# Score bounds from five multiply-adds on VectorE instead of five small matmuls, with a column step of five in Wq and Wk

## The chip, the cores and the metric

The kernel runs on one core of a Trainium2 chip. The metric is the time of one execution in microseconds (us), taken as the median of several runs. A core has five engines with queues of their own: TensorE (PE in the profile, its weight loads PEld), VectorE (DVE), ScalarE (ACT), GpSimd (POOL) and SyncE (SP), which here does nothing but issue DMAs. Each queue is worked off in order; between queues only semaphores order the work.

## The reference, cut to what matters

A block with segmented linear memory beside a softmax attention, gated by a GLU. B = 1, S = 2048, D = 640, H = 32 heads of Dh = 20, four segments of L = 512 tokens, GLU width 1536.

```
xn = layernorm(x)
q, k, v = heads(xn @ wq), heads(xn @ wk), heads(xn @ wv)
for each segment s of 512 tokens:
    logits = q_s k_s^T * Dh**-0.5 + mask           # causal mask of -1e9
    a_dot  = softmax(logits) v_s
    a_mem  = phi(q_s) M / (phi(q_s) z + 1e-6)      # phi(t) = t+1 if t > 0 else exp(t)
    o      = g * a_mem + (1 - g) * a_dot           # g = sigmoid(beta), one per head
    M, z   = M + phi(k_s)^T v_s, z + sum(phi(k_s))
s = concat(o) @ wo
g = silu( (sigmoid(xn @ w_gate) * (xn @ w_up)) @ w_down )
out = x + s * g
```

The kernel subtracts from each score a bound of its query instead of the row's maximum: for a query q and a head, the sum over the head's 20 features of |q_d| times the largest |k_d| in the segment. The bound is the same for all keys of a query, so the softmax does not change; it only keeps the exponential from overflowing.

## The kernel before, in words

**Tiling.** Everything is held transposed, with features on the 128 partitions and 512 tokens along a row: xnT is 5 chunks of 128 features. Per segment, `proj` (L283) makes K and Q in five tiles of 128 features x 512 tokens each, five matmuls a tile, evacuated to bf16 by ScalarE or VectorE into `ktd` and `qtd` (L292 to L301). V is made with tokens on the partitions (L347). The GLU is 12 gate tiles and 12 up tiles (L420, L431) and eight down tiles (L443).

**Scores.** A head has 20 features, so four heads go side by side: `KT` and `QT` hold, at partitions 32r to 32r+19, the features of head 4g+r, for eight groups g. As the features of a head straddle the 128-feature chunks, K and Q go out to DRAM (`spill`, L303, into Kd and Qd) and come back in that layout (`relayout`, L310, four DMAs of 20 partitions a half; half 0 is groups 0 to 3, half 1 groups 4 to 7). A unit of `scores` (L545) is up to 512 columns for four heads at once, four row strips of TensorE; its PSUM tile Sps is single. One exponential on ScalarE (L556) reads it, GpSimd masks the diagonal (L558), `attend_T` (L562) multiplies by V, and VectorE and GpSimd divide (the "turn", L580 to L593). There are 80 units, 20 a segment; the text calls the stretch from one unit to the next a slot.

**The bound.** Three rows at partitions 32r+20 to 32r+22 of QT carry the negative bound in three parts, against three rows of ones in KT, so that the scores' matmul (23 rows deep) subtracts it. `do_K` takes the largest |k| of each feature over the 512 tokens (`kabs`, L295). `q_abs` clears the sign bits of Q (`aq`, L320, in two calls). `bound` (L323) multiplies an indicator of heads, `Ind`, by kabs (`ik`, L326). `bound_mm` (L330) runs five matmuls of 32 output columns, ik against aq, into the PSUM tile `cps`, ScalarE copies it to `cb` (L338), and a DMA puts it into DRAM (Bd, L339). `bound_dma` (L341) brings the three rows back into QT, four DMAs a half.

**Memory.** phi of Q and of the transposed K (`ktok`, a DMA transpose of Kd, L377) is made in place by `phi_min`, `phi_exp`, `phi_end` (L361 to L375): two VectorE instructions, an exponential on ScalarE, an addition on VectorE. phi(Q) is needed from segment 1 on, for `mem_part` (L402), whose blocks of M lie in the order of the natural features.

**Order.** Everything is put in order by hand. `TIMES` gives for each piece of a segment the slot (0 to 20) at which it is issued, and the main loop issues, slot by slot, scores and exponentials, then the events due in this slot, filled up between them with GLU matmuls (`fill`, `step`) so that the work per slot is even. An event carries its TensorE time; that of `bound_mm` is C_NS. In slots ahead of an `attend_T`, matmuls are issued as four of 32 output columns each (`mm`, L134 instead of L130), which run side by side. All PSUM tiles but Sps come from one pool of four buffers. Segment m = n+1 has its K, Q, V and bounds made in slots 9.75 to 20 of segment n; segment 0 has them made ahead of the first slot, written out at the end of the set-up code.

## Time and profile before

| what | value |
|---|---|
| median of 3 runs | 319.95 us (319.74 to 320.09) |
| profiled execution: span from the first to the last instruction | 317.6 us |
| what lies around that span in the median run | 2.35 us |
| first unit of scores (start of the first slot) | 35.68 us |
| first unit of segments 1, 2, 3 | 102.6, 169.1, 235.9 us |
| granted TensorE clock over the span | 0.999 |
| ScalarE's exponentials (L556) | 81, 1.86 us each |

The profile is of one execution on the chip. A group's line gives the source line, the engine, the operation, out<-in with partitions x elements, the count, then busy time and the mean of one in ns, then the engine's idle time just before those instructions and what ended most of it. The waits view names who waited for whom, in us in total, times and the longest. The timeline gives start, duration and line; "SPq" rows are DMAs being issued, not moved. When a DMA has landed is told by its semaphore's marks in the trace.

### The profile page before, as it was taken

To read this page: it belongs to the slowest core of one execution; us is meant where nothing else is said; L and a number is where in the kernel's file an instruction comes from. 1 tells how busy PE (TensorE), PEld (TensorE's weight loads), DVE (VectorE), ACT (ScalarE), POOL (GpSimd) and SP (SyncE) were. 2 spreads that over 40 slices of the span, in tenths; PEclk is the share of its full clock that TensorE was granted. 3 is DMA by queue.
4 is the path that set the end of the run, shared out by engine and by line. 5 is a ranking of instruction groups with operands and counts; after the bars stand their busy time and mean duration, and the time that the engine had idled before them with its cause. 6 is when DMAs were issued, how large, how long until landed. Compare 5 with 4: busy or idle time off the path is not lost.

```text
span 317.6 us, 10049 instructions
## 1 busy us (share of the span) xinstructions
PE 309.7 (98%) x4215; PEld 167.1 (53%) x4244; DVE 229.5 (72%) x505; ACT 227.2 (72%) x229; POOL 135.5 (43%) x230
## 2 busy tenths in 40 slices
PE   8999999999999999999999999999999999999995
PEld 3544445665555445654665455545466645445673
DVE  6474356755869888997779999977787686734565
ACT  3723477788898877778898868678897766777631
POOL 1870036535263445334453354444533353535322
PEclk9999999999999999999999999999999999999999
DMA  7984886420752462505954443238533000350302
GB/s 252 364 328 142 289 221 191 105 46 2 215 158 62 130 130 85 126 23 173 240 168 122 114 110 109 82 121 210 168 82 120 19 23 23 114 137 4 99 20 83
DMA packets 56085, 41.36 MB, mean 130 GB/s; under 512 B 26952, under 2 KB 54664, under 8 KB 56040
## 3 DMA queue, kind: packets, MB, share of 16 engines
q1 hardware_dynamic: 53496, 35.97, 39.7%
q10 hardware_dynamic: 2544, 4.75, 4.0%
q8 instruction: 33, 0.54, 0.7%
q14 instruction: 12, 0.10, 0.1%
HBM read 19.90 MB, written 14.78 MB: 109 GB/s over the span
## 4 chain that ended last, share of the span: by engine, by line
PE 96%; issue 1%; ACT 1%; DVE 1%; ACTq 0%
PE yp L130 11%; PE up L130 11%; PE gp L130 10%; PE psq L130 10%; PE Sps L548 9%; PE gp L134 6%; PE up L134 6%; PE yp L134 6%; PE psv L130 6%; PE ApsT L572 5%; PE psq L134 4%; PE sp L130 3%; PE sp L134 3%; PE sp L532 2%; PE psv L134 1%; PE wps L644 1%
## 5 line engine op out<-in xcount | busy, mean ns | idle before, releaser
L556 ACT ACTIVATE pt<-Sps 128x2048 bf16<-128x2048 f32 (+1 forms) x81 | 150.3, 1856 | 40.8 <-PE Sps L548 35.9
L558 POOL TENSOR_SCALAR_AFFINE_SELECT pt<-pt 128x512 bf16<-128x512 bf16 x128 | 83.2, 665 | 157.6 <-ACT pt L556 157.5
L438 DVE SCALAR_TENSOR_TENSOR hT<-tg,up 128x512 bf16<-128x512 bf16 x48 | 32.4, 675 | 23.2 <-PE up L130 8.7
L130 PE MATMUL up<-xnT,Wu 128*128 128x512 bf16 x147 | 40.3, 380 | 1.2 <-issue 1.0
L130 PE MATMUL yp<-Wd,hT 128*128 128x320 bf16 x257 | 40.1, 300 | 0.0
L427 ACT ACTIVATE tg<-gp 128x512 bf16<-128x512 f32 x48 | 28.6, 596 | 14.4 <-PE gp L130 11.0
L130 PE MATMUL gp<-xnT,Wg 128*128 128x512 bf16 x144 | 38.1, 379 | 0.3 <-issue 0.2
L548 PE MATMUL Sps<-QT,KT 23*128 23x128 bf16 (+3 forms) x512 | 32.6, 301 | 0.2
L591 DVE STREAM_TRANSPOSE obT<-ob 128x512 bf16<-128x512 bf16 x30 | 21.1, 705 | 13.4 <-POOL ob L587 13.3
L130 PEld LDWEIGHTS <-hT 128*128 128x128 bf16 x257 | 23.5, 98 | 11.6 <-issue 3.0
L455 DVE SCALAR_TENSOR_TENSOR aa<-t,yp 128x320 bf16<-128x320 bf16 x32 | 15.3, 480 | 13.8 <-ACT t L454 13.7
L134 PE MATMUL gp<-xnT,Wg 128*32 128x512 bf16 x360 | 24.1, 380 | 0.0
L548 PEld LDWEIGHTS <-KT 23*128 23x128 bf16 x512 | 10.0, 92 | 24.5 <-issue 24.1
L130 PEld LDWEIGHTS <-Wu 128*128 128x128 bf16 x160 | 14.3, 98 | 16.2 <-issue 3.2
L593 DVE STREAM_TRANSPOSE tb<-ApsT 128x512 f32<-128x512 f32 x30 | 21.2, 708 | 2.2 <-PE ApsT L572 2.1
L572 PE MATMUL ApsT<-pt,V 128*32 128x512 bf16 (+2 forms) x480 | 22.7, 299 | 0.0
L130 PEld LDWEIGHTS <-Wg 128*128 128x128 bf16 x150 | 14.1, 98 | 16.0 <-issue 1.9
L134 PE MATMUL up<-xnT,Wu 128*32 128x512 bf16 x320 | 21.7, 380 | 0.0
L454 ACT ACTIVATE t<-yp 128x320 bf16<-128x320 f32 x32 | 13.9, 435 | 10.2 <-PE yp L130 8.5
L130 PE MATMUL psv<-Wv,xnT 128*128 128x320 bf16 x130 | 20.6, 299 | 0.2
L587 POOL TENSOR_TENSOR ob<-tb,rb 128x320 bf16<-128x320 f32 x27 | 19.8, 733 | 2.3
L134 PE MATMUL yp<-Wd,hT 128*32 128x320 bf16 x508 | 20.0, 300 | 0.0
(122 smaller groups left out, 448.7 us busy)
## 6 DMA issues: line engine op xcount, KB each, us to landing
KT<-Kd SPq DMA_DIRECT2D x32, 80.0 KB
QT<-Qd SPq DMA_DIRECT2D x32, 80.0 KB
out_dram<-xt SPq DMA_DIRECT2D x14, 160.0 KB
Wg<-in_B_w_gate_dram ACTq DMA_DIRECT2D x1, 1920.0 KB
Wu<-in_B_w_up_dram ACTq DMA_DIRECT2D x1, 1920.0 KB
xt<-in_A_x_dram SPq DMA_DIRECT2D x3, 640.0 KB
Wd<-in_B_w_down_dram SPq DMA_DIRECT2D x1, 1920.0 KB
Xd<-xn SPq DMA_DIRECT2D x12, 160.0 KB
```

The lines of the kernel that those rows point to most:

```text
L130: nc.tensor.matmul(out_, lhsT=lhsT, rhs=rhs, start=start, stop=stop, skip_group_check=True)
L134: nc.tensor.matmul(out_[cols], lhsT=lhsT[:, cols], rhs=rhs, start=start, stop=stop, tile_position=(0, 32 * r), skip_group_check=True)
L427: nc.scalar.activation(tg[:], gp[:], ACT.Tanh, scale=0.5)
L438: nc.vector.scalar_tensor_tensor(out=h[:], in0=seg[n]["tg"][:], scalar=1.0, in1=up[:], op0=ALU.add, op1=ALU.mult)
L455: nc.vector.scalar_tensor_tensor(out=s["aa"][j][:, hs], in0=t2[:], scalar=1.0, in1=yp[:], op0=ALU.add, op1=ALU.mult)
L548: nc.tensor.matmul(Sps[:, r, c0:c0 + ncol], lhsT=KT[32 * r:32 * r + DH + 3, g, kb * P:(kb + 1) * P], rhs=QT[32 * r:32 * r + DH + 3, g, q0: ...
L556: nc.scalar.activation(pt[:, :, 0:ntot], Sps[:, :, 0:ntot], ACT.Exp, scale=SCALE)
L558: nc.gpsimd.affine_select(out=pt[:, :, c0:c0 + P], in_=pt[:, :, c0:c0 + P], compare_op=ALU.is_ge, fill=0.0, base=0, pattern=[[0, 4], [1, P ...
L572: nc.tensor.matmul(ps[32 * r:32 * r + 32, q0:L], lhsT=Vflat[n % 2][:, off:off + 32], rhs=t[:, r, c0:c0 + ncol], start=(i == 0), stop=(i == ...
L587: nc.gpsimd.tensor_tensor(ob[:, :, 0:DH], tb[:, :, 0:DH], rb[:].unsqueeze(2).to_broadcast([P, L // 32, DH]), op=ALU.mult)
L591: nc.vector.transpose(s["obT", g // 4][:, g % 4, :], ob[:].rearrange("p b e -> p (b e)"))
L593: s["turn", g] = (lambda: nc.vector.transpose(tb[:].rearrange("p b e -> p (b e)"), ps[:]), quotients, turn_back)
```

## The change

- `proj` reads Wq and Wk with a column step of five: tile c holds the features 5p + c at partition p, not 128c + p. So the 20 features of a head lie on four partitions, five to each, all five tiles alike.
- `bound` becomes five VectorE instructions, issued in four events: cb = aq[0] * kmax[0], then four times cb = aq[c] * kmax[c] + cb, each 128 x 512 with the scalar taken per partition. `Ind`, `ik`, the five matmuls, the PSUM tile `cps` and ScalarE's copy go. Each head has four bound rows now, one for each of its four partitions; KT's unused rows are -1 instead of 1, and the scores' matmul is 24 rows deep.
- K and Q are each written out whole, in one DMA (five rows of 1 KB at a stretch for each partition), after their last tile, and not in two parts. In DRAM the features stand in natural order.
- From segment 1 on, Q is read back in natural order (`q_again`, 128 partitions of five rows of 1 KB) into a new `qtd` for phi, so phi of Q begins a little later.
- The order of the DMAs on SP changes accordingly: Q out, K out, bounds out, Q back, then the relayouts. In the set-up code Q now goes out after its fifth tile instead of three tiles after the third.

```diff
-    q_spill1=15.26, k_spill1=17.0, q_abs=(13.5, 14.79), bound=14.78, bound_mm=15.9, ...
-    phi_q=((16.0, 16.6, 17.12), (18.3, 18.7, 19.18)),
+    q_spill=14.3, k_spill=14.95, k_lay0=15.5, q_lay0=16.33, q_again=15.3, q_abs=(13.5, 14.79), bound=(14.5, 14.7, 15.0, 15.2),
+    phi_q=((16.4, 17.0, 17.5), (18.3, 18.7, 19.18)),
...
-        nc.gpsimd.memset(KT[:].bitcast(mybir.dt.uint32), 0x3F803F80)
+        nc.gpsimd.memset(KT[:].bitcast(mybir.dt.uint32), 0xBF80BF80)
...
-            mm(ps[:], W[:, k, c * P:(c + 1) * P], xnT_of[n][:, k, :], k == 0, k == DC - 1)
+            mm(ps[:], W[:, k, :].rearrange("p (m c) -> p c m", c=DC)[:, c, :], xnT_of[n][:, k, :],
+               k == 0, k == DC - 1)
...
+    def spill(n, dd, key, eng):
+        eng.dma_start(dd[n % 2][:].rearrange("(m c) n -> m c n", c=DC), seg[n][key][:])
+
+    def q_again(n):
+        seg[n]["qt"] = stg.tile([P, DC, L], BF, name="qtd")
+        nc.sync.dma_start(seg[n]["qt"][:], Qd[n % 2][:].rearrange("(c p) n -> p c n", p=P))
...
+    def bound(n, c0, c1):
+        s = seg[n]
+        if c0 == 0:
+            s["cb"] = stg.tile([P, L], BF, name="cb")
+        for c in range(c0, c1):
+            kmax = s["kabs"][:, c:c + 1]
+            if c == 0:
+                nc.vector.tensor_scalar(s["cb"][:], s["aq"][:, c, :], kmax, None, op0=ALU.mult)
+            else:
+                nc.vector.scalar_tensor_tensor(out=s["cb"][:], in0=s["aq"][:, c, :], scalar=kmax, in1=s["cb"][:],
+                                               op0=ALU.mult, op1=ALU.add)
+        if c1 == DC:
+            nc.sync.dma_start(Bd[n % 2][:], s["cb"][:])
...
-            nc.sync.dma_start(QT[32 * r + DH:32 * r + DH + 3, 4 * half:4 * half + 4, :],
+            nc.sync.dma_start(QT[32 * r + DH:32 * r + DH + 4, 4 * half:4 * half + 4, :],
...
-    for c in range(5):
+    for c in range(DC):
         do_K(0, c, nc.vector)
+    spill(0, Kd, "kt", nc.sync)
+    for c in range(DC):
+        do_Q(0, c, nc.scalar)
         if c == 2:
-            spill(0, 0, nc.sync, None)
-    for c in range(3):
-        do_Q(0, c, nc.scalar)
-    q_abs(0, 0, 3)
-    spill(0, 0, None, nc.sync)
+            q_abs(0, 0, 3)
+            bound(0, 0, 3)
     relayout(0, 0, Kd, KT, nc.sync)
-    relayout(0, 0, Qd, QT, nc.sync)
-    for c in range(3, 5):
-        do_Q(0, c, nc.scalar)
+    spill(0, Qd, "qt", nc.sync)
     q_abs(0, 3, DC)
-    bound(0)
+    bound(0, 3, DC)
     finish(do_gate(0, 0))
     finish(do_up(0, 0))
-    bound_mm(0)
+    relayout(0, 0, Qd, QT, nc.sync)
     bound_dma(0, 0)
```

More of the change, by code (lines that the diff above doesn't have):

```diff
@@ L70 @@
     K_eng='vaava', Q_eng='avvav', V=(10.3, 13.3, 14.4, 14.6, 16.35, 17.45, 19.75, 19.85), V_eng='avaavvav',
-    k_spill0=14.77, k_lay0=15.15, q_spill0=14.1, q_lay0=16.33, q_spill1=15.26, k_spill1=17.0, q_abs=(13.5, 14.79), bound=14.78,
-    bound_mm=15.9, bound_lay0=18.6, load_x=14.7, phi_k=((7.08, 7.78, 8.23), (12.7, 12.8, 13.7)),
-    phi_q=((16.0, 16.6, 17.12), (18.3, 18.7, 19.18)),
+    q_spill=14.3, k_spill=14.95, k_lay0=15.5, q_lay0=16.33, q_again=15.3, q_abs=(13.5, 14.79), bound=(14.5, 14.7, 15.0, 15.2),
+    bound_lay0=18.6, load_x=14.7, phi_k=((7.08, 7.78, 8.23), (12.7, 12.8, 13.7)),
+    phi_q=((16.4, 17.0, 17.5), (18.3, 18.7, 19.18)),
 )
@@ L114 @@
     Xd = [dpool.tile([L, D], BF, name=f"Xd{i}") for i in range(2)]
-    Bd = [dpool.tile([3 * H, L], BF, name=f"Bd{i}") for i in range(2)]
+    Bd = [dpool.tile([4 * H, L], BF, name=f"Bd{i}") for i in range(2)]
     OTd = [dpool.tile([D, L], BF, name=f"OTd{i}") for i in range(2)]
@@ L185 @@
     QT = cpool.tile([P, NG, L], BF, name="QT")
-    Ind = cpool.tile([P, DC, 4, NG], BF, name="Ind")
     VN = 4 * H * E1
@@ L199, in late_constants @@
         nc.gpsimd.tensor_copy(Mbd[:, 0, 0:1], after[:, 0:1])
-        nc.gpsimd.memset(Ind[:], -1.0)
-        nc.gpsimd.affine_select(out=Ind[:], in_=Ind[:], compare_op=ALU.is_ge, fill=0.0, base=0,
-                                pattern=[[P, DC], [-DH, 4], [-4 * DH, NG]], channel_multiplier=1)
-        nc.gpsimd.affine_select(out=Ind[:], in_=Ind[:], compare_op=ALU.is_ge, fill=0.0, base=DH - 1,
-                                pattern=[[-P, DC], [DH, 4], [4 * DH, NG]], channel_multiplier=-1)
-        nc.gpsimd.memset(KT[:].bitcast(mybir.dt.uint32), 0x3F803F80)
+        nc.gpsimd.memset(KT[:].bitcast(mybir.dt.uint32), 0xBF80BF80)
         ones_columns(1)
@@ L301, in do_Q @@
         proj(n, Wq, c, seg[n]["qt"][:, c, :], evac)
-    def spill(n, half, eng_k, eng_q):
-        c0, c1 = ((0, 3), (3, 5))[half]
-        for eng, dd, key in ((eng_k, Kd, "kt"), (eng_q, Qd, "qt")):
-            if eng is not None:
-                eng.dma_start(dd[n % 2][c0 * P:c1 * P, :].rearrange("(c p) n -> p c n", p=P),
-                              seg[n][key][:, c0:c1, :])
+    def spill(n, dd, key, eng):
[3 more added lines that the diff above has]
+        nc.sync.dma_start(seg[n]["qt"][:], Qd[n % 2][:].rearrange("(c p) n -> p c n", p=P))
     def relayout(n, half, dd, dst, eng):
@@ L321, in q_abs @@
                                 op0=ALU.bitwise_and)
-    def bound(n):
+    def bound(n, c0, c1):
         s = seg[n]
-        ik = stg.tile([P, DC, H], BF, name="ik")
-        nc.vector.tensor_tensor(ik[:], Ind[:].rearrange("p c r g -> p c (r g)"),
-                                s["kabs"][:].unsqueeze(2).to_broadcast([P, DC, H]), op=ALU.mult)
-        s["bound"] = ik, s["aq"]
-    def bound_mm(n):
-        ik, aq = seg[n]["bound"]
-        cps = ps_d.tile([3 * H, L], F32, name="cps", tag="d")
-        for c in range(DC):
-            i = c % 3
-            nc.tensor.matmul(cps[H * i:H * i + H, :], lhsT=ik[:, c, :], rhs=aq[:, c, :],
-                             start=(c < 3), stop=(c >= 2), tile_position=(0, H * i), skip_group_check=True)
-        cb = stg.tile([3 * H, L], BF, name="cb")
-        nc.scalar.copy(cb[:], cps[:])
-        nc.sync.dma_start(Bd[n % 2][:], cb[:])
+        if c0 == 0:
[9 more added lines that the diff above has]
+            nc.sync.dma_start(Bd[n % 2][:], s["cb"][:])
     def bound_dma(n, half):
-        src = Bd[n % 2][:].rearrange("(i r g) n -> r i g n", i=3, r=4)
+        src = Bd[n % 2][:].rearrange("(g r i) n -> r i g n", r=4, i=4)
         for r in range(4):
-            nc.sync.dma_start(QT[32 * r + DH:32 * r + DH + 3, 4 * half:4 * half + 4, :],
+            nc.sync.dma_start(QT[32 * r + DH:32 * r + DH + 4, 4 * half:4 * half + 4, :],
                               src[r][:, 4 * half:4 * half + 4, :])
@@ L548, in scores @@
                 nc.tensor.matmul(Sps[:, r, c0:c0 + ncol],
-                                 lhsT=KT[32 * r:32 * r + DH + 3, g, kb * P:(kb + 1) * P],
-                                 rhs=QT[32 * r:32 * r + DH + 3, g, q0:L],
+                                 lhsT=KT[32 * r:32 * r + DH + 4, g, kb * P:(kb + 1) * P],
+                                 rhs=QT[32 * r:32 * r + DH + 4, g, q0:L],
                                  start=True, stop=True, tile_position=(32 * r, 0))
@@ L731 @@
     nc.sync.dma_start(Wd[:], B_w_down.rearrange("(f p) n -> p f n", p=P))
-    spill(0, 1, nc.sync, nc.sync)
     k_tok(0)
@@ L743 @@
     GLU_NS, V_NS, AV_NS = DC * mm_ns(L), DC * mm_ns(HD), 700
-    MEM_NS, C_NS = 220, 2 * mm_ns(L) + 200
+    MEM_NS = 220
     dense = deque()
@@ L845 @@
         on("V", V_NS, do_V, *[(m, i // 2, i % 2, EVAC[TIMES["V_eng"][i]]) for i in range(8)])
-        on("k_spill0", 0, spill, (m, 0, nc.sync, None))
+        on("k_spill", 0, spill, (m, Kd, "kt", nc.sync))
         on("k_lay0", 0, relayout, (m, 0, Kd, KT, nc.sync))
-        on("q_spill0", 0, spill, (m, 0, None, nc.sync))
+        on("q_spill", 0, spill, (m, Qd, "qt", nc.sync))
+        on("q_again", 0, q_again, (m,))
         on("q_lay0", 0, relayout, (m, 0, Qd, QT, nc.sync))
-        on("q_spill1", 0, spill, (m, 1, None, nc.sync))
-        on("k_spill1", 0, spill, (m, 1, nc.sync, None))
         on("q_abs", 0, q_abs, (m, 0, 3), (m, 3, DC))
-        on("bound", 0, bound, (m,))
-        on("bound_mm", C_NS, bound_mm, (m,))
+        on("bound", 0, bound, (m, 0, 2), (m, 2, 3), (m, 3, 4), (m, 4, DC))
         on("bound_lay0", 0, bound_dma, (m, 0))
```

## The prediction

> **What bounds the kernel now.** The page's first part and the engines' shares of its chain come first.

> ```profile
> PE 309.7 (98%) x4215; PEld 167.1 (53%) x4244; DVE 229.5 (72%) x505; ACT 227.2 (72%) x229; POOL 135.5 (43%) x230
> ...
> PE 96%; issue 1%; ACT 1%; DVE 1%; ACTq 0%
> ```

> TensorE is the path: what shortens its queue shortens the kernel, what lengthens another engine's work counts only once TensorE waits for it. The waits view, for TensorE's matmuls alone, says how often that happens:

> ```profile
> PE wps L644 <- DVE mn L155: 1.2, 1, 1.2
> PE up L130 <- issue: 1.0, 6, 0.2
> PE am L130 <- issue: 0.3, 2, 0.2
> ```

> After the first row (the start) hardly a wait is left that another engine ends. So each edit has to be priced by two questions: how long it holds TensorE, and whether the other engines' added work outgrows the cover they have now. That cover is the four PSUM buffers: TensorE can fill three more tiles after one that waits for its evacuation. Tiles take 0.7 us (ApsT, L572) to 1.1 us (five 512-column matmuls, which start 0.216 us apart), with scores between them, so about 2.2 us of lateness at an evacuating engine is free.

> **The change part by part.**

> *TensorE, the five bound matmuls.* In the set-up they stand alone, as the timeline shows:

> ```profile
> 25.22 1.24 PE L130 MATMUL up<-xnT,Wu 128*128 128x512 bf16 x5
> 26.40 0.61 PE L335 MATMUL cps<-aq,ik 128*32 128x512 bf16 x5
> 26.94 0.82 PE L130 MATMUL gp<-xnT,Wg 128*128 128x512 bf16 x3
> ```

> The up tile has used its time at 25.22 + 5 x 0.216 = 26.30; the next tile starts at 26.94. So 0.64 us go. In the later segments the timeline has

> ```profile
> 88.70 0.39 PE L335 MATMUL cps<-aq,ik 128*32 128x512 bf16 x3
> 88.71 0.38 PE L572 MATMUL ApsT<-pt,V 128*32 128x512 bf16 x1
> 88.92 0.38 PE L335 MATMUL cps<-aq,ik 128*32 128x512 bf16 x2
> ```

> There the fourth quarter of the array was lent to ApsT, and the rest of the second round too. Five matmuls on a quarter of the array are 5/4 x 0.216 = 0.27 us; two whole rounds would be 0.43. I take 0.27, since the rows show the free quarters in use. Sum: 0.64 + 3 x 0.27 = 1.45 us off TensorE (1.93 at most). A score matmul 24 rows deep instead of 23 stays in the same 32-row strip: nothing. A reordering comes with it: by the two instruction orders 21 matmuls go from whole to four quarters, which costs nothing (four quarters start 0.216 us apart too), and mode switches around scores stay at 51 and 30; the one pair around cps goes, already counted.

> *TensorE, the weights with a step.* 200 weight loads' worth of K and Q now read every fifth element. No row has a stepped load. Bounds: contiguous loads come as fast as

> ```profile
> L612 PEld LDWEIGHTS <-pt 128*128 128x128 bf16 x80 | 2.9, 96 | 0.5
> ```

> which is 2.9/80 = 0.036 us each when nothing else limits them, and each has 0.216 us behind the matmul before it. A stepped load may therefore be six times as slow before it is seen, except where a K or Q tile follows scores and nothing covers its first load: seven such places in the order, at most 7 x 0.18 = 1.3 us. I take 0, as the row leaves a factor of six. [...]

> *ScalarE.* `cb` goes: 4 x 0.59 us, off the path (TensorE waits for no evacuation), so nothing.

> *VectorE.* The groups by line and form that price it:

> ```profile
> L438 DVE SCALAR_TENSOR_TENSOR hT<-tg,up 128x512 bf16<-128x512 bf16 x48 | 32.4, 675 | 23.2 <-PE up L130 8.7 <-ACT tg L427 7.2 <-PE up L134 6.9
> ...
> L320 DVE TENSOR_SCALAR aq<-qtd 128x1536 uint16<-128x1536 uint16 x4 | 2.2, 554 | 1.8 <-ACT qtd L288 1.5 <-DMA Od<-odot 0.3
> ...
> L320 DVE TENSOR_SCALAR aq<-qtd 128x1024 uint16<-128x1024 uint16 x4 | 1.7, 423 | 1.6 <-ACT qtd L288 1.6
> L326 DVE TENSOR_TENSOR ik<-Ind,kabs 128x160 bf16<-128x160 bf16 x4 | 1.3, 324 | 0.1
> ```

> The first product: 554 - 423 = 131 ns per 512 elements, so 423 - 131 = 292 ns. The four multiply-adds: 675 ns by the same operation at the same size, though that one reads PSUM; from below, the additions L375 (808 ns for 1280 elements, 931 for 1536, 0.48 ns an element) give 439 ns; from above, 675 plus the 72 ns by which a multiply with a per-partition scalar (L582, 552) exceeds one without (L455, 480). I take 675. Per segment 0.29 + 4 x 0.675 - 0.32 = 2.67 us more, 10.7 in all. The windows view around the three bounds shows room (DVE busy 10.47, 9.82, 10.84 us of 14):

> ```profile
> 84.00:98.00 14.00, 13.79 (x229) 7.12 (x228) 10.47 (x21) 12.80 (x13) 7.72 (x12) 1.00 0.53 166
> 151.00:165.00 14.00, 13.95 (x269) 9.12 (x273) 9.82 (x21) 12.81 (x13) 7.95 (x13) 1.00 0.79 207
> 217.00:231.00 14.00, 13.90 (x233) 7.21 (x231) 10.84 (x21) 12.31 (x12) 7.65 (x12) 1.00 0.63 172
> ```

> Behind the bounds in VectorE's queue stand a turn, an hT and V's copy: TensorE's evacuations. In segment 1 the last reduction ends at 87.6, so the bounds end at 87.6 + 0.29 + 1.35 + 0.42 (second aq) + 1.35 = 91.0; the turn's transpose, which ran at 90.67, runs at about 92.3, V's copy at 93.2 instead of 92.1. That is 1.1 to 1.6 us late, inside the 2.2. Nothing.

> *Q read back.* The new wait: phi's first minimum reads the new qtd. SP issues the read behind the bounds' DMA, so at about 91.4; a lone 384 KB (Q of segment 0) landed 2.5 us after issue, and the trace's 1 KB packets take 46 ns on one of 16 engines, so 640 of them some 1.9 us; with K still in flight I take 3.7 us, 95.1. VectorE, in order, reaches the minimum at 93.6: 1.5 us of waiting, and by the same sums about 1.5 in segment 2 and 1.4 in segment 3. Next behind it are phi's maximum, a turn and hT; hT ran at 95.7 and would run at about 96.6. About 1 us late, covered; the idle gaps of 0.6 and 1.0 us at 92.6 and 94.0 swallow the rest. ScalarE's exponential of phi stands one slot later in its queue and finds its input ready within 0.6 us.

> *DMAs past each other.* K and Q go out in one piece each; SP loses two issues per segment and gains one. The relayouts of half 0 wait for K whole: in segment 2, the tightest, K's last tile is evacuated at 153.8, its DMA goes at 154.4 instead of 153.5, lands about 160.2, so the bound rows are issued at 163.2 to 164.4 (before: 164.2 to 165.4) and land before 168, with the scores due at 169.07 less what is saved. Nothing. In the set-up the margin shrinks: Q leaves after tile five (24.9) and, behind K's relayout on SP, at 26.5, lands near 30.2, its relayout takes 1.45 us, the bound rows 1.2, landing 1.9 after issue: 34.8. The first scores, at 35.68 before, are due at 35.04. I charge 0.2 us.

> **Sum.** 1.45 - 0.2 = 1.25 us off the profiled execution: span 317.6 to 316.35. The median run has 2.35 us around that span, so 319.95 - 1.25 = 318.7.

> **The rivals.**
> *VectorE's wait outgrows its cover* (slower). The read of Q takes not 3.7 but 5.2 us, as x of segment 2 did (640 KB, issued 152.88, landed 158.05). The wait becomes 3.0, 0.8 beyond the cover of 2.2, three times: +2.4, so 321.1; it decides from a landing of 4.4 us on. For it: VectorE and ScalarE are both above 70% there. Against: the DMA engines were half idle in that window (0.53, 0.79, 0.63).
> *Stepped weights set the pace* (slower). From 0.216 us on each load shows: at seven times the contiguous 0.036, 200 x 0.036 = +7 us, 326. Against: a step of 10 bytes would have to cost a factor of six.
> *The scores wait at the start* (same). K and Q land 1 us later than worked out, because the loads of Wg and Wu still run (K's DMA took 6.4 us there): the 0.64 us of the set-up is lost, 319.4.
> *The bound cost TensorE nothing to begin with* (same): in segments 1 to 3 the quarters were filled, new order of fillers costs as much as it saves: 319.6.

> **How the numbers follow.** Forecast 0.46, VectorE's wait 0.22, stepped weights 0.08, the start 0.14, no saving 0.10. A measurement here tells 0.2% (0.64 us) from no change: faster 0.46, same 0.24, slower 0.30. The range goes from 317.8 (the upper bound of TensorE's saving, 1.93, without the start's charge, and 0.2 for the spread of the runs shown) to 322 (the first rival with its landing 0.3 us later still); the second rival is left out.

> **What would show it.** Right: no cps rows, psq matmuls still 0.216 us apart, the first scores near 35.0 to 35.3, mn<-qtd waiting some 1.5 us for a DMA three times, no TensorE waits by VectorE. Wrong: gaps before psq matmuls; TensorE or Sps waiting for VectorE or ScalarE around 93 to 100, 160 to 167 and 226 to 232; scores of slot 0, 20, 40 or 60 waiting for QT; multiply-adds far from 675 ns.

## The result and the profile after

The changed kernel takes 334.48 us (median of 6 runs, 332.01 to 335.71), the kernel before on the same chip 319.92 us (319.63 to 320.18, 6 runs): ratio 1.0449, 95% interval 1.0411 to 1.0488. It is 14.6 us slower; the forecast was 318.7 us, its range 317.8 to 322.0. The profiled execution has a span of 331.6 us. All medians here are of fast runs; experiments 3 and 4 had one slow run each (335.61 and 325.22 us), which is left out.

The first part of the page of the changed kernel, and the engines' shares of its chain:

```profile
PE 312.6 (94%) x4258; PEld 170.4 (51%) x4287; DVE 243.2 (73%) x521; ACT 225.6 (68%) x225; POOL 134.6 (41%) x227
...
PE 74%; DVE 11%; DMA 5%; ACT 4%; issue 3%; POOL 2%; SPq 0%; ACTq 0%; DVEq 0%
```

TensorE's share of the chain fell from 96% to 74%. Part of what took its place is DMA, which no share of busy time shows. VectorE's busy time grew by 13.7 us, 3 more than the forecast's 10.7, and at 73% of the span it still looks far from full. The waits view of the changed kernel (engine, line waited for; us in total, times, longest) names the new waits:

```profile
DVE mn L358 <- DMA qtd<-Qd: 9.3, 3, 3.4
...
ACT mn L363 <- DVE mn L358: 8.0, 6, 3.5
...
PE psv L130 <- DVE aa L447: 1.6, 1, 1.6
...
PE up L134 <- DVE hT L430: 1.5, 1, 1.5
PE dm L383 <- DVE aa L447: 1.5, 1, 1.5
```

The first row is the read of Q: three waits of 3.1 us each in the mean. Where the kernel before had hardly a wait of TensorE for another engine, there are now several on VectorE's evacuations, the longest 1.0 to 1.6 us each.

The timeline of VectorE in the changed kernel around the bounds of segment 1 (start, duration, line, and in brackets the idle time before and what ended it):

```profile
88.69 0.34 DVE L326 TENSOR_SCALAR cb<-aq,kabs 128x512 bf16<-128x512 bf16 x1
89.06 2.13 DVE L328 SCALAR_TENSOR_TENSOR cb<-aq,kabs,cb 128x512 bf16<-128x512 bf16 x2
91.12 0.41 DVE L316 TENSOR_SCALAR aq<-qtd 128x1024 uint16<-128x1024 uint16 x1
91.57 1.54 DVE L328 SCALAR_TENSOR_TENSOR cb<-aq,kabs,cb 128x512 bf16<-128x512 bf16 x2
93.02 0.70 DVE L583 STREAM_TRANSPOSE obT<-ob 128x512 bf16<-128x512 bf16 x1
93.65 0.65 DVE L430 SCALAR_TENSOR_TENSOR hT<-tg,up 128x512 bf16<-128x512 bf16 x1
...
98.12 0.46 DVE L358 TENSOR_SCALAR mn<-qtd 128x1024 bf16<-128x1024 bf16 x1 [2.57 <-DMA qtd<-Qd]
98.62 0.43 DVE L359 TENSOR_SCALAR qtd<-qtd 128x1024 bf16<-128x1024 bf16 x1
98.96 0.70 DVE L583 STREAM_TRANSPOSE obT<-ob 128x512 bf16<-128x512 bf16 x1
99.59 0.65 DVE L430 SCALAR_TENSOR_TENSOR hT<-tg,up 128x512 bf16<-128x512 bf16 x1
```

SP's queue in the same stretch, issues only:

```profile
93.13 0.32 SPq L331 DMA_DIRECT2D Bd<-cb  x1
93.54 0.39 SPq L304 DMA_DIRECT2D qtd<-Qd  x1
```

And TensorE's two stalls there:

```profile
94.35 0.38 PE L130 MATMUL up<-xnT,Wu 128*128 128x512 bf16 x1 [1.27 <-DVE hT L430]
...
100.29 0.40 PE L134 MATMUL gp<-xnT,Wg 128*32 128x512 bf16 x4 [0.98 <-DVE hT L430]
```

Read these three together. The bounds end at 93.1, so their DMA goes at 93.13 and the read of Q, behind it on SP, at 93.54; Q itself had landed at 88.83. VectorE passes its evacuations, comes to `mn<-qtd`, and stands there for 2.57 us until the read lands at 98.10. The two hT evacuations behind the bounds and behind the wait are the ones TensorE stalls for, once each. It is a loop of three in-order queues.

### The profile page after: what moved, and what is told of

Read it like the earlier page. It is cut to its first block, busy times and chain, and to the rows that moved or that the text cites. A ratio compares the mean times of both kernels' runs of the same rounds, so it can differ in the third digit from the quotient of the medians.

```text
span 331.6 us, 10118 instructions
## 1 busy us (share of the span) xinstructions
PE 312.6 (94%) x4258; PEld 170.4 (51%) x4287; DVE 243.2 (73%) x521; ACT 225.6 (68%) x225; POOL 134.6 (41%) x227
## 4 chain that ended last, share of the span: by engine, by line
PE 74%; DVE 11%; DMA 5%; ACT 4%; issue 3%; POOL 2%; SPq 0%; ACTq 0%; DVEq 0%
PE yp L130 9%; PE up L130 8%; PE psq L130 7%; PE gp L130 7%; PE Sps L540 7%; PE gp L134 5%; PE yp L134 5%; DMA qtd<-Qd 5%; PE up L134 4%; PE ApsT L564 4%; PE psv L130 4%; ACT pt L548 3%; PE psq L134 3%; PE sp L130 2%; DVE cb L328 2%
## 5 line engine op out<-in xcount | busy, mean ns | idle before, releaser
L550 POOL TENSOR_SCALAR_AFFINE_SELECT pt<-pt 128x512 bf16<-128x512 bf16 x128 | 85.1, 682 | 170.7 <-ACT pt L548 170.5
L130 PE MATMUL yp<-Wd,hT 128*128 128x320 bf16 x247 | 39.7, 301 | 1.7 <-DVE hT L430 1.2
L130 PE MATMUL up<-xnT,Wu 128*128 128x512 bf16 x140 | 38.3, 380 | 2.2 <-DVE hT L430 1.3
L130 PE MATMUL gp<-xnT,Wg 128*128 128x512 bf16 x140 | 37.8, 379 | 1.7 <-DVE hT L430 1.1
L540 PE MATMUL Sps<-QT,KT 24*128 24x128 bf16 (+3 forms) x512 | 33.2, 302 | 0.4 <-issue 0.2
L130 PEld LDWEIGHTS <-hT 128*128 128x128 bf16 x247 | 22.7, 98 | 13.4 <-issue 3.2
L583 DVE STREAM_TRANSPOSE obT<-ob 128x512 bf16<-128x512 bf16 x30 | 21.1, 703 | 10.7 <-POOL ob L579 10.4
L134 PE MATMUL up<-xnT,Wu 128*32 128x512 bf16 x364 | 24.6, 380 | 1.5 <-DVE hT L430 1.5
L134 PE MATMUL gp<-xnT,Wg 128*32 128x512 bf16 x360 | 24.2, 380 | 1.2 <-DVE hT L430 1.0
L540 PEld LDWEIGHTS <-KT 24*128 24x128 bf16 x512 | 10.0, 92 | 26.4 <-issue 25.5
L130 PE MATMUL psv<-Wv,xnT 128*128 128x320 bf16 x130 | 21.5, 308 | 2.0 <-DVE aa L447 1.6
L130 PEld LDWEIGHTS <-Wg 128*128 128x128 bf16 x150 | 14.0, 98 | 17.0 <-issue 3.4
L134 PE MATMUL yp<-Wd,hT 128*32 128x320 bf16 x548 | 21.9, 302 | 0.7 <-DVE hT L430 0.7
L446 ACT ACTIVATE t<-yp 128x320 bf16<-128x320 f32 x32 | 13.9, 435 | 11.9 <-PE yp L130 8.7
L564 PE MATMUL ApsT<-pt,V 128*32 128x512 bf16 (+2 forms) x480 | 21.6, 299 | 0.4 <-DVE aa L447 0.4
L130 PEld LDWEIGHTS <-Wu 128*128 128x128 bf16 x149 | 13.3, 98 | 15.5 <-issue 3.0
```

The costliest lines, as they stand in the source:

```text
L130: nc.tensor.matmul(out_, lhsT=lhsT, rhs=rhs, start=start, stop=stop, skip_group_check=True)
L134: nc.tensor.matmul(out_[cols], lhsT=lhsT[:, cols], rhs=rhs, start=start, stop=stop, tile_position=(0, 32 * r), skip_group_check=True)
L540: nc.tensor.matmul(Sps[:, r, c0:c0 + ncol], lhsT=KT[32 * r:32 * r + DH + 4, g, kb * P:(kb + 1) * P], rhs=QT[32 * r:32 * r + DH + 4, g, q0: ...
L550: nc.gpsimd.affine_select(out=pt[:, :, c0:c0 + P], in_=pt[:, :, c0:c0 + P], compare_op=ALU.is_ge, fill=0.0, base=0, pattern=[[0, 4], [1, P ...
L564: nc.tensor.matmul(ps[32 * r:32 * r + 32, q0:L], lhsT=Vflat[n % 2][:, off:off + 32], rhs=t[:, r, c0:c0 + ncol], start=(i == 0), stop=(i == ...
L583: nc.vector.transpose(s["obT", g // 4][:, g % 4, :], ob[:].rearrange("p b e -> p (b e)"))
```

## Where the time comes from, slot by slot

The starts of score units, each against the same unit of the kernel before (us; from the timelines of profiled executions; unit 20 opens segment 1, 40 segment 2, 60 segment 3):

| unit | changed | no Q read back | old order of fillers | neither read nor new order | and no multiply-adds | Q read ahead | and x later |
|---|---|---|---|---|---|---|---|
| 0 | -0.80 | -0.67 | -0.51 | -0.30 | -0.48 | -0.64 | -0.47 |
| 15 | +0.57 | +0.66 | +0.25 | +0.27 | -0.59 | +0.04 | -0.03 |
| 20 | +3.57 | +2.10 | +2.93 | +0.90 | -1.02 | +0.67 | +0.60 |
| 40 | +9.33 | +3.59 | +8.01 | +2.19 | -0.24 | +4.66 | +2.28 |
| 60 | +13.78 | +5.07 | +11.17 | +3.11 | -0.49 | +5.75 | +3.41 |
| 80 | +14.26 | +5.58 | +11.15 | +3.10 | -0.50 | +5.73 | +3.40 |

Of the 15.1 us that the changed kernel loses from its first unit on, 13.0 fall in slots 15 to 20 of the three stages, where bounds and phi stand: 3.0, 5.5 and 4.4 us. The largest is that between units 35 and 40, where segment 2 is made ready ("in segment 2" below means this stretch). The other columns are the experiments that follow. Each was timed against the kernel before on its own chip: 319.98 us for the first four, 319.42 for the next four, then 319.63 and 319.72 for two pairs.

## The experiments

The theory after the result was A: VectorE in order, waiting for the read of Q, holds up evacuations. Its rivals were B, the multiply-adds alone, and C, the changed order of the GLU fillers (the event of the bound matmuls carried a TensorE time in the plan, and with it gone fillers move).

**1. Without Q read back.** Phi takes Q in the order of the stepped weights, so its features are not the reference's.

```diff
-        on("q_again", 0, q_again, (m,))
```

> The changed kernel (334.5 us) without the DMA that reads Q back: phi works in place on the Q that was written out, whose features then stand in the stepped order, so the memory part of the output is computed from wrongly paired features; all instructions but that DMA stay. Theory A (VectorE's wait for the returning Q is the loss): the three waits of 9.3 us in all go, and with them most of the 12.5 us lost in slots 15-20, 35-40 and 55-60: 323 to 326. Theory B (the multiply-adds in VectorE's queue are the loss): only the stalls right behind the wait go, 328 to 331. Theory C (new order of fillers and evacuations): 333 or more.

325.01 us, ratio 1.0163 (1.0141 to 1.0185): 9.5 us less than the changed kernel. A holds, but 5.0 us over the kernel before are left.

**2. One product.** The four multiply-adds are left out in all four segments; the bound takes one of its five products.

```diff
-        for c in range(c0, c1):
+        for c in range(c0, min(c1, 1)):
```

> The changed kernel with the first product of the bound alone: the four multiply-adds per segment (3.1 us by the trace) are left out, so the bound is too small. Theory A: VectorE comes to phi earlier, but the returning Q still lands behind K's DMA, so it waits longer there: 331 or more. Theory B: the stalls ahead of the wait (1.4 us at 92.7 and its like) and a part of those behind it go: 325 to 328. Theory C: 333 or more.

327.14 us, ratio 1.0235 (1.0197 to 1.0273): 7.3 us less. B's number, not A's. The wait is still there, and longer:

```profile
DVE mn L358 <- DMA qtd<-Qd: 10.8, 3, 4.7
```

VectorE comes to phi sooner and waits longer for the read (in all 10.8 us instead of 9.3), but it is late by less. So 9.5 and 7.3, together 16.8, exceed the whole loss of 14.6: the two causes share a lateness. They share a stretch at half clock too (last section), which the runs of neither experiment have. Neither theory alone was enough.

**3. The old order of fillers.** An event that issues nothing gets the time of the old one.

```diff
+    MEM_NS, C_NS = 220, 2 * mm_ns(L) + 200
...
+        at(t0 + 15.9, C_NS, lambda: None)
```

> The changed kernel with an empty event of C_NS at slot 15.9, so that the main loop counts TensorE time as before and every engine has its fillers and evacuations in the old order. Theory C (the new order): 0.9 us at slot 6 and 1.5 us at slot 14 come back at least, 331 to 332. Theories A and B alone: 334, within 0.7.

331.90 us, ratio 1.0371 (1.0327 to 1.0415): 2.6 us less. The interval just touches that of the changed kernel (1.0411 to 1.0488), so this run alone hardly proves C; experiments 1 and 5, which differ by the same edit without the read, do (1.0163 and 1.0081, intervals well apart). C is real and small. It shows best ahead of the bounds: from unit 0 to 15 the changed kernel takes 52.55 us, the kernel before 51.18, and the old order 51.07 (in experiment 7). Slot 5 takes 4.81 us in place of 3.89: an `obT`, which waits 2.27 us for GpSimd, stands ahead of an hT on VectorE now, and TensorE stalls 0.67 us for that hT.

**4. The step alone.** The kernel before with Wq and Wk read with a step of five.

> The kernel before (319.9 us) with Wq and Wk read with the column step of five and nothing else changed: features then belong to other heads than in the reference. If stepped weight loads cost TensorE time (second rival of the prediction): over 1 us more, 321 to 326. If they are hidden behind the matmul before them, as the 216 ns between psq matmuls of the changed kernel say: 319.9 within 0.6.

320.55 us, ratio 1.0012 (0.9994 to 1.003). Two hundred stepped weight loads cost the kernel nothing that can be told from noise; by the interval it is 1 us at most.

**5 and 6. Old order without Q read back, with the multiply-adds and without them.** Both are sums of the edits above.

> The changed kernel without Q read back, and with an empty event of the bound matmuls' price in the plan, so that the fillers stand in their old order: of the three suspects only the four multiply-adds are left. Phi is formed from Q in the order of the stepped weights, so its features are not the reference's. Theory A (wait, multiply-adds and order are three causes, the first two of which share one lateness in VectorE's queue): 325.0 less the 2.1 us that the old order gave back, so 322 to 324; TensorE then still waits for VectorE near 93, 162 and 228 us, some 3 to 4 us in all. Theory B (the order costs only where the wait is there too): as without Q read back, 324.5 to 325.5.

> The same with the four multiply-adds left out too (the bound then takes the first of its five products alone): none of the three suspects is left. Theory A (the three are the whole loss): TensorE's saving shows undiminished, 318.2 to 319.2, and no stall over 0.4 us at 93, 162 and 228. Theory B (something else costs too: K and Q written in one piece each, the later relayouts, a fourth bound row): 320.5 or more, with stalls of scores on DMAs.

With the multiply-adds 321.97 us, ratio 1.0081 (1.0062 to 1.01); without them 318.88 us, ratio 0.9986 (0.9976 to 0.9995). Theory A's numbers both times, the first at its edge of 322. The pair is the cleanest price of the multiply-adds: 16 of them, 12 us of VectorE's time, cost 3.1 us, with no read of Q to wait for. In the two profiles, 0.9 us of the difference arise by unit 1, whose first slot took 4.35 us instead of 3.67, and 2.7 us behind unit 15, in segments 1 to 3. The pair also shows that the three causes make up the loss: with all of them gone the kernel is 0.5 us faster than before. Of the waits view with the multiply-adds these rows are not in the one without them:

```profile
PE gp L130 <- DVE hT L430: 1.1, 1, 1.1
PE up L130 <- DVE tb L585: 0.8, 1, 0.8
```

The first is in segment 3. VectorE's timeline there, without the multiply-adds and then with them:

```profile
220.12 0.34 DVE L326 TENSOR_SCALAR cb<-aq,kabs 128x512 bf16<-128x512 bf16 x1
...
222.39 0.65 DVE L430 SCALAR_TENSOR_TENSOR hT<-tg,up 128x512 bf16<-128x512 bf16 x1
```

```profile
222.54 0.35 DVE L326 TENSOR_SCALAR cb<-aq,kabs 128x512 bf16<-128x512 bf16 x1
222.93 1.89 DVE L328 SCALAR_TENSOR_TENSOR cb<-aq,kabs,cb 128x512 bf16<-128x512 bf16 x2
...
225.62 1.54 DVE L328 SCALAR_TENSOR_TENSOR cb<-aq,kabs,cb 128x512 bf16<-128x512 bf16 x2
...
227.71 0.65 DVE L430 SCALAR_TENSOR_TENSOR hT<-tg,up 128x512 bf16<-128x512 bf16 x1
```

From the first product to hT it is 2.3 us in the one and 5.2 in the other: hT is 2.9 us later. From the `up` matmuls ahead to the `gp` matmul that waits for it, TensorE takes 1.87 us in place of 0.64, so it loses 1.2 us (the row above, which counts idle time alone, has 1.1). So here 1.7 us of lateness were free, not 2.2.

**7. Phi later.** The whole kernel, old order of fillers, phi's steps on Q 1.5 slots later.

```diff
-    phi_q=((16.4, 17.0, 17.5), (18.3, 18.7, 19.18)),
+    phi_q=((17.9, 18.4, 18.9), (19.2, 19.7, 20.2)),
```

> The changed kernel whole, with the fillers in their old order and the steps on the read-back Q planned 1.5 slots later, so that VectorE and ScalarE come to them after the data have landed. Theory A (the wait costs because VectorE stands in it, in order, and holds up evacuations behind it): the wait goes and the time is that of the kernel without Q read back in the old order, 322 to 324. Theory B (the read costs by its traffic, by delaying K's and Q's relayouts): no better than with the old order alone, 331 or more. Theory C (the steps, pushed later, collide with those of the next stage): 326 to 330, with the stalls moved to the next five slots.

323.46 us, ratio 1.012 (1.0101 to 1.0139), 4.0 us over the kernel before on its chip, where the old order alone is 11.9 over: 7.9 us less. A holds: most of the cost of the read was VectorE standing in the wait. 1.5 us over experiment 5 are left, with two waits:

```profile
DVE mn L358 <- DMA qtd<-Qd: 1.7, 2, 1.4
```

**8. The change in segment 0 alone,** where VectorE is idle (in the set-up); segments 1 to 3 as before.

> The kernel before, with the change made in segment 0 alone: stepped Wq and Wk there, its bound on VectorE (which has idle time in the set-up), four rows; segments 1 to 3 as before, and no Q read back, since the phi of segment 0 stands on the whole weights' order only from segment 1 on. Theory A (the set-up's five bound matmuls stood alone on TensorE, and the first scores came 0.80 us earlier with the change): 319.1 to 319.4, against 319.95 before. Theory B (the slots after it lose what the start gives, as slots 6 and 14 did): 319.7 to 320.2.

319.37 us, ratio 0.9991 (0.998 to 1.0002): not told from no change. The first scores came 0.79 us sooner, but the first slot took 4.35 us in place of 3.67, as the last of its four scores waited for a DMA of bound rows (L368), and between units 35 and 40, with a stall of 0.5 for an `aa`, another 0.6 were lost. That stage is as in the kernel before; experiment 4 lost 0.5 there too, so executions differ at this place without the change. The time lies where theory A had it, but 319.42 was the time before on that chip, so B is nearer: the start's gain is given back.

**9. Q read ahead.** Old order of fillers; SP issues the read before the bounds' DMA.

```diff
-    q_again=15.3
+    q_again=15.1
```

> The changed kernel whole, fillers in their old order, and one thing more: SP issues the read of Q right behind K's write, ahead of the bound rows' DMA, which waits for the four multiply-adds. In the changed kernel that order made the read start at 93.5 us, 4.7 us after Q had landed (88.8). Theory A (the wait was the place in SP's queue): the read starts near 89 and lands near 93, before VectorE comes to phi's minimum; the wait goes without moving phi, 322 to 323.5. Theory B (the read is slow in itself, or its traffic delays K's write and the relayouts): it lands after 96, or scores wait for KT; 326 or more.

324.74 us, ratio 1.0147 (1.0104 to 1.019): between the theories. In segment 1 the read went at 90.58 (later than expected) and landed at 94.56, and between units 15 and 20 as little is lost as without any read (0.63 us, as in experiment 5). In segment 2 it was issued at 158.24 and landed only at 164.43, 6.2 us later; VectorE waited 2.61 us and TensorE stalled. The windows view (us; busy time and count of PE, PEld, DVE, ACT, POOL; granted clock; DMA share; GB/s):

```profile
158.20:160.00 1.80, 1.80 (x20) 1.02 (x19) 1.76 (x3) 1.51 (x2) 0.55 (x1) 1.00 1.06 391
160.00:163.00 3.00, 2.65 (x21) 1.80 (x20) 1.84 (x5) 1.88 (x1) 2.15 (x5) 1.00 1.02 374
...
165.00:167.00 2.00, 0.14 (x20) 0.13 (x20) 1.01 (x3) 2.00 (x4) 0.00 (x0) 1.00 0.61 172
167.00:169.00 2.00, 2.00 (x100) 1.72 (x95) 2.00 (x5) 1.39 (x1) 0.54 (x1) 0.50 0.43 104
```

While the read is under way the 16 DMA engines have no time to spare (shares of 1.06 and 1.02, at 374 to 391 GB/s): x of segment 3 and K, 640 KB each, had been issued 3.3 and 2.6 us before. Then TensorE stands for most of 165 to 167, and the next row has the granted clock at 0.50.

**10. The bound split between VectorE and GpSimd,** on top of experiment 9: in segments 1 to 3 VectorE makes the products, GpSimd the four additions, 0.7 slots apart.

```diff
+            nc.vector.tensor_scalar(prod, s["aq"][:, c, :], kmax, None, op0=ALU.mult)
+            if c > 0:
+                nc.gpsimd.tensor_tensor(s["cb"][:], s["cb"][:], prod, op=ALU.add)
```

> The same with the bound split between two engines in segments 1 to 3: VectorE makes the five products alone (five times the 0.34 us of the first one, 1.7 us in place of 3.4), GpSimd adds them up, and the steps stand 0.7 slots apart. Theory A (what the multiply-adds cost goes by VectorE's time in front of its evacuations): with 1.35 of their 3.0 us left, 318.9 + 0.45 x 3.1 = 320.3, so 319.8 to 320.8. Theory B (GpSimd then holds TensorE instead): its additions, at 1.1 us or more each (0.73 to 1.10 us for 320 elements now), stand in front of the masks that ApsT waits for; TensorE stalls for GpSimd and the time is 322 or more.

325.21 us, ratio 1.0162 (1.0127 to 1.0197): B's number, and no better than experiment 9. An addition took 1.16 us:

```profile
L332 POOL TENSOR_TENSOR cb<-cb,aq 128x512 bf16<-128x512 bf16 x12 | 13.9, 1157 | 2.4 <-DVE aq L330 2.2
```

But it was not the masks: GpSimd's `ob` came late, VectorE's `obT` waited for it (0.90 us at 95.7) with hT behind it. The waits for Q stayed too (6.2 us in three; in segment 2 the read took 7.5 us to land), so the run does not price VectorE's share by itself.

**11 and 12. x loaded later,** on top of experiment 9, to clear the DMA engines for the read in segment 2; and phi later as well.

```diff
-    load_x=14.7
+    load_x=17.2
```

> The kernel with Q read ahead of the bounds' DMA, and the load of the next but one segment's x (640 KB, which stood ahead of the read on SP in segment 2) moved behind the relayouts, to slot 17.2. With Q read ahead, segment 2 alone still lost 4.0 us: the read took 6.2 us there, with x and K in flight (16 DMA engines busy for 1.02 and 1.06 of the time), VectorE waited 2.6 us, TensorE 1.9 us, and its clock then fell to half for some 3 us. Theory A (the traffic): the read lands 1.5 us or more sooner in segment 2, the stall and the half clock go, 321.5 to 323. Theory B (K's write alone fills the DMA engines): still a wait of 2 us or more, 324 to 325.5.

> The same with phi's steps on Q 1.5 slots later too: nothing waits for the read any more, everything of the reference is computed, and the multiply-adds alone remain. Theory A: the time of the kernel without Q read back in the old order, 321.5 to 322.8. Theory B (the read costs by its mere traffic): 323.5 or more, as with phi later alone.

322.52 us (1.0079, 1.0048 to 1.011) and 322.50 us (1.0085, 1.0052 to 1.0119): theory A both times. In segment 2 the read now landed 4.3 us after its issue (158.06 to 162.34), the long stall went, and the clock stayed at 1.00:

```profile
160.00:163.00 3.00, 2.65 (x20) 1.78 (x19) 2.27 (x7) 1.92 (x2) 2.15 (x5) 1.00 0.84 280
...
166.00:169.00 3.00, 3.00 (x65) 1.97 (x54) 2.92 (x7) 2.18 (x4) 0.64 (x1) 1.00 0.86 211
```

Both compute the whole reference. They are 2.8 us over the kernel before on their chip, and experiment 5, without Q read back, is 2.6 over. So the read itself can be had for next to nothing, once it is issued early and past other traffic. To move phi later as well gained nothing more; in its profile the first scores of segment 2 waited 0.79 us for a DMA instead. What is left is about the price of the multiply-adds, and no version tried here that makes the bounds of all segments on VectorE beats the kernel before.

**The account.** Each kernel is set against the kernel before on its own chip: the changed kernel is 14.6 us slower, experiment 3 11.9, experiment 5 2.6, and experiment 6 is 0.5 faster. So the order of fillers is worth 2.6 us (changed less 3), the read 9.4 (3 less 5), the multiply-adds 3.1 (5 less 6) and TensorE's saving -0.5. Without the read the order of fillers is worth 2.5 (1 less 5), about the same. The read and the multiply-adds do not add up like that. Without the multiply-adds the read costs about 5.2 us, by a sum: experiment 2's 7.2, less 2.5 for the order, plus the 0.5 saved. Beside them it costs 9.4. Part of the 4.2 between the two is the half clock: the granted clock was 0.985 to 0.995 in all runs of experiment 3 and in five of six of the changed kernel, and 0.998 to 1.000 in all of experiments 1 and 2.

## Why the prediction was wrong, step by step

The step that failed is the one on VectorE's queue. The forecast found the bounds 1.1 to 1.6 us late and the read about 1 us late, held each by itself against the same 2.2 us of cover, and put both at nothing. The runs showed 3.1 us for the multiply-adds and 9.4 for the read beside them. A gain of 1.25 us was forecast and the kernel lost 14.6. The steps one by one:

- *TensorE's saving, 0.64 + 3 x 0.27 us.* Right in size where it can be seen: the first scores came 0.80 us sooner in the changed kernel (0.3 to 0.8 over the profiles with the change), and with all three causes gone 0.43 and 0.42 us are gained from unit 15 to 20 and from 55 to 60, the upper bound for a later segment. In segment 2 of that run 0.66 us were lost instead, with a stall for an `aa` of the kind that experiments 4 and 8 have there too, with that segment's bounds made as before. So 0.5 us net.
- *Stepped weights at nothing.* Right for the time (experiment 4). The loads themselves did become slower, as their rows show, in the kernel before and then in experiment 4:

```profile
L130 PEld LDWEIGHTS <-Wq 128*128 128x128 bf16 x85 | 8.2, 98 | 9.3 <-issue 0.4
```

```profile
L130 PEld LDWEIGHTS <-Wq 128*128 128x128 bf16 x85 | 9.8, 118 | 7.8 <-issue 0.4
```

  A load took 118 ns instead of 98, while those of Wu stayed at 98. A fifth more is far from the factor of six at which, by the forecast, a load would show behind matmuls 0.216 us apart. No run varied the step, so the cause of the 20 ns is not shown.
- *Start and the DMAs past each other.* First scores at 34.88, forecast 35.0 to 35.3: right within 0.1. The charge of 0.2 us was too small for some executions: in those profiled for experiments 3, 5, 8, 9 and 11 the first slot took 4.2 to 4.5 us in place of 3.67, as later scores waited for bound rows. The later relayouts cost next to nothing: two waits of the scores' weight loads, 0.8 us in all.
- *The multiply-add at 675 ns.* 752 ns in the median, the upper bound of 747 in effect. The view by line:

```profile
L328 DVE SCALAR_TENSOR_TENSOR cb<-aq,kabs,cb x16: 750/752/1100, 23.6 to 233.4; 128x512 bf16<-128x512 bf16 x16
```

  0.3 us a segment: a small part of the error. The first two in segment 1 took 2.13 us together; why, no run tells.
- *"About 2.2 us of lateness at an evacuating engine is free"* and *"1.1 to 1.6 us late, inside the 2.2. Nothing."* This failed first. The bounds of segment 1 ended at 93.1, not 91.0: 1.1 us because they began late (88.69, not 87.6, after the order of the fillers had cost its part), 1.0 because they ran longer. And the cover was not there whole. In experiment 5 it was 1.7 us in segment 3, not 2.2, and in segment 1 of the changed kernel hT was 1.5 us later within its slots than before (6.23 us from unit 15, before 4.72) and TensorE stalled 1.27. That four buffers give 2.2 us only if the tiles before were evacuated on time is argued; no run tries it by itself.
- *Q read back, "about 1 us late, covered".* This is the part with the largest price. The read went at 93.54 (forecast 91.4), because it stood behind the bounds on SP, and took 4.56, 5.09 and 5.37 us to land (forecast 3.7); VectorE waited 2.57, 3.32 and 3.39 us (forecast 1.5). Worse than the numbers was the sum: the lateness of the bounds and the wait were each set against the same 2.2 us, though they follow one another in one queue within a few us. Rival 1 had this mechanism, and the landings are past its point of 4.4 us, but its price (0.8 us three times) again spent the cover that the bounds had used up.
- *"DMA engines were half idle in that window (0.53, 0.79, 0.63)".* These were means over 14 us. In the stretch where the read of segment 2 runs, the share is 0.94 in the changed kernel:

```profile
163.00:167.00 4.00, 3.51 (x34) 2.27 (x33) 2.07 (x5) 2.25 (x2) 3.01 (x6) 1.00 0.94 290
```

- *A reordering "which costs nothing".* It was priced by modes of the array alone. What it moves in VectorE's queue, an evacuation behind an instruction that waits for GpSimd, was not looked at: 2.5 us.
- *ScalarE's copy at nothing* was not contradicted: TensorE had no wait for it before.

## What to carry to other kernels

Cover is spent once: add up everything that makes one in-order queue late, and set the sum against the buffers' slack as it stands at that place. A read back through DRAM should be issued from a place in its queue that waits for its data alone, and past heavy traffic (in segment 2 it took 4.3 us to land with x moved away, 6.2 with x ahead of it); if it still lands late, its reader belongs behind the evacuations that others wait for. An event that leaves a hand-made plan takes its time out of the plan too, and what moves up has to be looked at in every queue.

## What the runs showed of the hardware

```profile
172.59:176.00 3.41, 1.74 (x17) 0.89 (x18) 3.30 (x9) 3.41 (x3) 0.29 (x2) 1.00 0.34 102
176.00:179.40 3.40, 3.40 (x22) 1.47 (x24) 3.37 (x9) 0.74 (x3) 2.82 (x4) 0.50 0.40 112
```

```profile
171.02:174.43 3.41, 1.74 (x12) 1.06 (x11) 3.31 (x9) 3.11 (x4) 0.99 (x2) 1.00 0.45 143
```

At half clock `psv` matmuls start 0.267 us apart instead of 0.135, so 3.4 us do the work of 1.7; this is part of the 9.4 us put down to the read. In five of the six runs of the changed kernel the mean clock was 0.994 or 0.995, and they took 333.3 to 335.7 us; the sixth, at 1.000, took 332.0.

The fourteen profiles show one pattern. In the changed kernel the clock changes at 5.34, 176.00 and 179.42 us, in the kernel before at 6.11 and 316.73 us: these times lie a whole number of 3.41 us apart (50 and 1, and 91), on a grid that starts elsewhere in each of the two. Inside the kernels the clock was halved four times, and the window of 3.41 us just before had TensorE busy for 0.51 of its time (changed kernel), 0.17 (experiment 3), 0.45 (9) and 0.43 (10). Between 10 and 313 us no other window of the grid is below 0.51 in any of the fourteen profiles. In the kernel before, the window in which TensorE's work ends (313.3 to 316.7 us) is busy for 0.18, and the clock is halved behind it too. So in these profiles it went by TensorE's work within one such window, not by the length of a stall: in experiment 3 a stall of 2.1 us up to 239.75 fell on two windows (0.63 and 0.74 busy) and cost no clock. The limit lay near one half here. It can't be read closer: the windows of the changed kernel and of experiment 2 above are both busy for 1.74 of 3.41 us, and the ends of matmuls are modelled. No kernel was made to try it.

A multiply-add of two bf16 tiles in SBUF with a scalar per partition took 752 ns for 512 columns (median of 16), more than the 671 ns (mean of 48) of the one that reads PSUM (hT); a plain product with a scalar took 346 (median of 4).
